# Threshold attention and a GELU feed-forward on one core: the last six token blocks by 49 products, eight blocks in pairs, merged additions, and one written order for every task

## The chip, the cores and the metric

The kernel runs on one core of a Trainium2 chip. The core has five engines with a queue of instructions each: TensorE (PE, the matrix multiplications; the loading of its weights is shown apart, as PEld), VectorE (DVE), ScalarE (ACT), GpSimd (POOL) and SyncE (SP, which here only starts transfers). The engines run side by side and wait for each other by semaphores; 16 DMA engines move data. The metric is the time of one execution on the device in microseconds (us).

## The reference

All numbers are 32-bit floats. Attention with a threshold is followed by a feed-forward:

```python
q, k, v: (8, 8, 576, 64)                     # batch, heads, positions, head size
scores = scale * q @ k.T                     # per batch and head: 576 x 576
keep   = scores >= max(scores, row) - tau    # everything else gets -1e9
attn   = exp(kept scores - max) / (sum + 1e-9)
x = (attn @ v)  as  (4608 tokens, 512)       # 8 batches x 576 positions, 8 heads x 64
h = x @ w_in                                 # w_in  512 x 2048
g = h * sigmoid(1.702 * h)
out = g @ w_out                              # w_out 2048 x 512
```

## The kernel before

**Attention.** Two heads of a batch are done together, so there are 32 "pairs" n (4 per batch). Each uses the four quarters of TensorE's array, 64 rows by 64 columns, for four small multiplications side by side. Pair n runs through these steps (functions of the code, whose lines are listed below): `load_qk`, `load_v` (transfers); `prep` (DVE transposes of q and k, L556); `scores` (PE, 9 groups of four 64x288 matmuls); `keep` (ACT copies the scores from PSUM to SBUF, L607) into five tiles t = 0 to 4, four of 128x1152 numbers and a last one of 128x576; `in_groups` (DVE maximum, L613), `over_tiles`, `cross_max` (ACT), `over_halves` and `spread_max`, which end in the row maximum spread over a tile called `mb`; `sub` (DVE subtracts `mb` from each of the five tiles, L687); `mask` and `exps` (ACT, L694 and L698); `in_groups` again for the sums; `values` (PE, L709); and `place_x` (DVE, L813), which divides by the sums and writes the pair's part of x, transposed, to the tile `xT`. The `values` of one pair and the `scores` of the next are interleaved on PE tile by tile in a run of about 8 us. In pairs 1 and 3 to 6 the subtraction of tiles 3 and 4 is not done by DVE but by a transfer that adds as it writes (`add_row`, L678), issued on POOL's queue.

**Feed-forward.** The 4608 tokens are 18 blocks of 256, numbered 0 to 17 here. Blocks 0 and 1 are done plainly. Others use Strassen's scheme: a product of two 2x2 block matrices takes seven products P1 to P7 instead of eight, at the price of additions of quarters of the operands and of the results.

- `seven` (blocks 2 to 6, and 13): first layer `product1` (L954), matmuls with 128 columns; each result of a half y is kept by ACT (`keep1`) or added by DVE (`add1`), and `silu1` (ACT) follows.
- `seven4` (blocks 7 to 12, in pairs, since two blocks share a weight): `product4` (L1127) with 256 columns, `keep4` (L1168), `add4` (L1173), `silu4`. The sums of weights that it needs are kept in DRAM (`wrow`) and are brought into four places in turn by transfers on POOL's queue (`w_flow`, L1104).
- Second layer of all of these: `product` (L1431), 256 columns, with sums of g made by DVE (`s_sums`, `s_minus`, `s_last`), and results read by `read` (ACT, L1446) and added into `osb` by DVE (L1453).
- `tail_blocks` (blocks 14 and 15, then 16 and 17): the scheme is applied twice, 49 products for each layer and pair of blocks, 128 columns each: `product2` (L1278) and `product3` (L1387). The 49 weights are sums made earlier on DVE (`scrap_sum`, named in EARLY_EXTRAS and LATE_EXTRAS) and written to DRAM (`ext`, `exu`), from where SP brings them back in time (`extra_in`, `extra2_in`).

**Order.** The program is built as a list of tasks (engine, cost, rank, what must be done first, places taken and given back). `run_in_order` goes through simulated time: whenever an engine is free it takes the ready task with the lowest rank. Feed-forward tasks on PE have the rank LAST, so attention comes first where it can; the others have ranks by pair, shifted by tables of numbers (EARLY, SECOND, LATER, CV). `limits` gives how many buffers of a kind there are. LEAD = 8 keeps pair n from starting before task `ffn[16 * (n - 8)]` of the feed-forward. What comes out is a fixed queue of instructions for each engine.

## Time and profile before

| what | value |
|---|---|
| time, median of 3 runs | 1224.76 us (1223.8 to 1225.64) |
| profiled execution: span | 1224.7 us |
| PE busy | 1206.5 us (99%) |
| DVE busy | 1077.1 us (88%) |
| ACT busy | 797.6 us (65%) |
| POOL busy | 69.3 us (6%) |
| mean traffic with memory | 111 GB/s |
| PE clock granted | full from the second 50 us on, 0.97 in the first |

The profile is that of one execution; its span is the time of that execution, and it lies at the median of the runs to 0.1 us. A busy share is a mean over stages with different limits, so the page's numbers are read stage by stage. A row of the groups ("by line") reads: line, engine, operation, output<-input with their shapes, how many, then busy us and mean ns of one, then the idle time of the engine just before them and what ended it. A row of windows gives the stretch, its length, each engine's busy us with the number of instructions, the clock, the busy share of the DMA engines and GB/s.

### The profile page before, as it was taken

Reading aid. Unit: us, or ns where it says so; the run is one execution under the profiler, and the core shown is the slowest. Engines: PE = TensorE matmul, PEld = TensorE weight load, DVE = VectorE, ACT = ScalarE, POOL = GpSimd, SP = SyncE. Lnnn points to the kernel's source line nnn. Section 1 sums busy time; section 2 is a strip of 40 time slices with the busy share of each in tenths; the row PEclk is TensorE's granted clock in tenths of the full one; section 3 lists DMA queues with packets and bytes.
Section 4 is the critical chain, followed back from the end, with each engine's and each line's share of the span. In section 5 each row is a group of like instructions: output and inputs, shape, how many; then the busy total and the mean of one; then the engine's idle time right before and its main releaser. Section 6 shows DMA issues by size and latency. Waiting matters only on the chain.

```text
span 1224.7 us, 26240 instructions
## 1 busy us (share of the span) xinstructions
PE 1206.5 (99%) x10672; PEld 995.8 (81%) x10672; DVE 1077.1 (88%) x1683; ACT 797.6 (65%) x1197; POOL 69.3 (6%) x114
## 2 busy tenths in 40 slices
PE   8999999999999999999999999999999999999998
PEld 5656777797978888888777777787787797999998
DVE  6989998878898998898699977998799989999797
ACT  6999977675765766684686468756875676340340
POOL 0111231100000000000100010001100000000000
PEclk9999999999999999999999999999999999999999
DMA  8957769492323241224423252225322351444443
GB/s 222 249 108 190 173 142 170 103 210 65 93 50 110 49 120 48 75 72 135 101 67 99 66 133 72 59 77 128 92 49 67 87 139 39 139 129 140 140 137 104
DMA packets 201193, 136.09 MB, mean 111 GB/s; under 512 B 146864, under 2 KB 163376, under 8 KB 200944
## 3 DMA queue, kind: packets, MB, share of 16 engines
q1 hardware_dynamic: 189712, 110.21, 34.0%
q0 software_dynamic: 10672, 23.90, 9.4%
q8 instruction: 84, 1.38, 0.5%
q10 hardware_dynamic: 688, 0.30, 0.1%
q14 instruction: 37, 0.30, 0.1%
HBM read 103.28 MB, written 23.75 MB: 104 GB/s over the span
## 4 chain that ended last, share of the span: by engine, by line
PE 88%; ACT 8%; DMA 2%; DVE 1%; issue 1%; SPq 0%; DVEq 0%; ACTq 0%
PE ops L1431 28%; PE pv L709 10%; PE ps L590 10%; PE hps L954 7%; PE hps L1127 7%; PE ps L954 5%; PE ps L1127 5%; PE hps L1278 4%; PE ops L1387 4%; PE ps L1278 3%; PE ps L1387 3%; ACT arena L698 2%; ACT arena L694 2%; PE hps L886 2%; ACT arena L607 2%; DMA arena<-in_moe_w_in_dram 1%
## 5 line engine op out<-in xcount | busy, mean ns | idle before, releaser
L613 DVE TRANSPOSE_TENSOR_REDUCE part<-arena 128x36 f32<-128x1152 f32 x300 | 363.8, 1239 | 52.6 <-ACT arena L607 40.2
L607 ACT COPY arena<-ps 128x576 f32<-128x576 f32 x288 | 171.2, 642 | 95.6 <-PE ps L590 95.5
L694 ACT ACTIVATE arena<-arena 128x1152 f32<-128x1152 f32 (+1 forms) x160 | 164.6, 1064 | 66.6 <-DVE arena L687 66.2
L1431 PE MATMUL ops<-w_out,arena 128*128 128x256 f32 x896 | 203.0, 381 | 0.1
L1431 PEld LDWEIGHTS ops<-w_out,arena 128*128 128x128 f32 x896 | 168.5, 190 | 28.5 <-issue 5.3
L687 DVE TENSOR_TENSOR arena<-arena 128x1152 f32<-128x1152 f32 (+1 forms) x150 | 180.9, 1241 | 0.7
L698 ACT ACTIVATE arena<-arena,shift 128x1152 f32<-128x1152 f32 (+1 forms) x160 | 179.7, 1156 | 1.4
L590 PE MATMUL ps<-arena 64*64 64x288 f32 x2304 | 172.1, 408 | 8.0 <-ACT arena L607 6.1
L709 PE MATMUL pv<-arena 64*64 64x288 f32 x2176 | 159.2, 405 | 0.0
L590 PEld LDWEIGHTS ps<-arena 64*64 64x64 f32 x2304 | 81.9, 132 | 71.5 <-ACT arena L607 29.7
L1431 PE MATMUL ops<-arena 128*128 128x256 f32 x576 | 129.1, 379 | 0.0
L709 PEld LDWEIGHTS pv<-arena 64*64 64x64 f32 x2176 | 80.3, 133 | 53.0 <-issue 9.0
L1431 PEld LDWEIGHTS ops<-arena 128*128 128x128 f32 x576 | 109.2, 190 | 15.8 <-issue 0.9
L1292 ACT COPY arena<-hps 128x512 f32<-128x512 f32 x44 | 25.7, 584 | 59.5 <-PE hps L1278 59.5
L632 ACT ACTIVATE other<-red,minus_gap 32x18 f32<-32x18 f32 x118 | 36.2, 307 | 35.1 <-DVE red L622 33.6
L1104 POOL DMA_DIRECT2D arena<-wrow x36 | 19.5, 540 | 619.0 <-DVE arena L1197 321.8
L886 PE MATMUL hps<-xT,w_in 128*128 128x256 f32 x232 | 51.2, 381 | 0.9 <-DVE arena L892 0.9
L886 PEld LDWEIGHTS hps<-xT,w_in 128*128 128x128 f32 x232 | 43.6, 190 | 8.6 <-DVE arena L892 1.5
L1453 DVE SCALAR_TENSOR_TENSOR osb<-ops,osb 128x256 f32<-128x256 f32 x98 | 39.2, 411 | 11.5 <-PE ops L1431 10.5
L954 PEld LDWEIGHTS hps<-xT,w_in 128*128 128x128 f32 x384 | 44.2, 192 | 1.5 <-issue 0.9
L954 PE MATMUL hps<-xT,w_in 128*128 128x128 f32 x384 | 45.3, 276 | 0.0
L1127 PE MATMUL hps<-xT,w_in 128*128 128x256 f32 x192 | 43.4, 379 | 0.0
(228 smaller groups left out, 1859.9 us busy)
## 6 DMA issues: line engine op xcount, KB each, us to landing
arena<-in_v_dram SPq DMA_DIRECT2D x128, 144.0 KB
arena<-exu SPq DMA_DIRECT2D x42, 256.0 KB
arena<-ext SPq DMA_DIRECT2D x39, 256.0 KB
arena<-wrow POOLq DMA_DIRECT2D x36, 256.0 KB, 3.3
arena<-in_k_dram SPq DMA_DIRECT2D x112, 72.0 KB
arena<-in_q_dram SPq DMA_DIRECT2D x112, 72.0 KB
out_dram<-osb SPq DMA_DIRECT2D x28, 256.0 KB
arena<-row_s SPq DMA_DIRECT2D x48, 144.0 KB
```

Of the source, the lines that this page charges most:

```text
L590: nc.tensor.matmul(ps[ts(c, KT), h, 0:SH], lhsT=mats[n, 1][ts(h, D), ts(j, KT)], rhs=mats[n, 0][ts(h, D), ts(c, SH)], start=True, stop=True,)
L607: nc.scalar.copy(out=sT[n, t][:, u], in_=pss.pop((n, j))[:, :, 0:SH])
L613: nc.vector.tensor_reduce(out=stats[n, op][:, t * 2 * QB : min(2 * t + 2, NK) * QB], in_=sT[n, t].rearrange("p u h (g d) -> p (u h g) d", ...
L687: engine.tensor_tensor(out=s, in0=s, in1=mbs[n].unsqueeze(1).to_broadcast(list(s.shape)), op=ALU.add if n in BY_DMA else ALU.subtract,)
L694: nc.scalar.activation(out=s, in_=s, func=AF.Prelu, alpha=STEEP)
L698: nc.scalar.activation(out=s, in_=s, func=AF.Exp, scale=SCALE, bias=shift)
L709: nc.tensor.matmul(o[c][ts(h, D), 0:SH], lhsT=left(j, h)[ts(c, KT)], rhs=sT[n, t][ts(c, KT), u, h, :], start=(j == 0), stop=(j == NK - 1),)
L886: nc.tensor.matmul(hidden[j][:, ts(i, BLK)], lhsT=w_in[:, c, ts(j, P)], rhs=xTs[i][:, c, :], start=(c == 0), stop=(c == NDC - 1), skip_gro ...
L954: nc.tensor.matmul(o[:, ts(j, HT)], lhsT=left[:, c, ts(4 * y + j, P)], rhs=right[:, c, :], start=(x in (P1, P2, P5) and j + c == 0), stop= ...
L1127: nc.tensor.matmul(o[:, ts(j, BLK)], lhsT=left[:, c, ts(j, P)], rhs=right[:, c, :], start=(x in (P1, P2, P5) and j + c == 0), stop=(j + c ...
L1278: nc.tensor.matmul(o[:, ts(j, HT)], lhsT=left[:, ts(j, P)], rhs=right, start=(m in (P1, P2, P5) and j == 0), stop=(j == 3), skip_group_che ...
L1431: nc.tensor.matmul(banks[blk][k][:, ts(o, HM)], lhsT=left[:, j, :], rhs=right[:, j, :], start=(j == 0), stop=(j == HF - 1),)
```

## The change

What it does, part by part:

1. **The tail grows from four blocks to six.** TAIL is NBLK - 6, so blocks 12 to 17 form three pairs with 49 products per layer. All three are created after the last pair of heads. x of blocks 12 to 15 is written to DRAM (`x_out`, on SP's queue) when it is complete and fetched back (`x_in`, SP) before its pair of blocks begins.
2. **Blocks 4 to 11 go in pairs** (`seven4`): WIDE_AT is (4, 6, 8, 10). Only blocks 2 and 3 remain with `seven`. EARLY_EXTRAS and LATE_EXTRAS spread the same 42 sums of weights over other blocks.
3. **P7 comes before P5** in the first layer (ORDER7), so that P4 stands between P5 and P3.
4. **Additions are merged.** `add1`, `add4`, `s_sums`, `s_next`, `s_minus`, `s_last`, `s_second` work on both halves at once (128x1024 instead of two of 128x512); `prep` transposes q and k at once; in pairs from 7 on the sums of tiles 1 and 2 come from one instruction; P4 is kept by an ACT copy like P1, P6 and P7, and all of a layer's silu come together at its end, 1024 wide.
5. **Pairs 7 to 31 leave the subtraction of tiles 3 and 4 to transfers.** The maximum is made negative (NEGATED), and `add_mb` issues on POOL's queue two transfers per pair that add `mb` (in SBUF) to tile 3 (576 KB) and tile 4 (288 KB).
6. **Buffers and gates.** The spread sums of pairs 7 to 31 have a place of their own ("rc2"); LEAD is NP, so that gate never closes; `values` may begin after two tiles' exps for all pairs after 7.
7. **A place for every task.** PLACES holds 4767 numbers, a permutation, one for each task; in `run_in_order` it replaces every rank. Pools and dependencies work as before.

Where the queues move, PE first: the start of a pair of blocks in the first layer, with a run of the attention (L709 and L590 before, L983 and L839 now). `hps` and `ps` are results in PSUM; a row with `x8` is one product of a half. Before:

```order
L1127 MATMUL hps<-xT,w_in 128x256 x8
L1127 MATMUL ps<-xT,w_in 128x256 x8
L1127 MATMUL hps<-arena_90,arena 128x256 x8
L709 MATMUL pv<-arena_90 64x288 x8
L590 MATMUL ps<-arena_90 64x288 x8
```

```order
L590 MATMUL ps<-arena_90 64x288 x4
L1127 MATMUL ps<-arena_90,arena 128x256 x8
L1127 MATMUL hps<-xT,w_in 128x256 x8
L1127 MATMUL hps<-arena_90,w_in 128x256 x8
L1127 MATMUL ps<-xT,arena 128x256 x8
```

Now (L1411 is `product4`):

```order
L1411 MATMUL hps<-xT,w_in 128x256 x8
L1411 MATMUL ps<-xT,w_in 128x256 x8
L1411 MATMUL hps<-arena_90,arena 128x256 x8
L1411 MATMUL hps<-xT,w_in 128x256 x8
L983 MATMUL pv<-arena_90 64x288 x8
L839 MATMUL ps<-arena_90 64x288 x8
```

P6 and P7 (the third and fourth row, both into `hps`) now follow each other, as P7 and P4 did before; the run of the attention stands one product later.

Then DVE in one pair's softmax, from `over_halves` on. Before, the five `sub` (L687) stand among the additions of the second layer (L1453) and `place_x` (L813):

```order
L639 SCALAR_TENSOR_TENSOR red<-red,gap,other_83 128x18
L651 STREAM_TRANSPOSE arena_90<-red 128x576
L687 TENSOR_TENSOR arena_90<-arena_90 128x1152
L1453 SCALAR_TENSOR_TENSOR osb<-ops,osb 128x256
L687 TENSOR_TENSOR arena_90<-arena_90 128x1152
L813 TENSOR_TENSOR xT<-pv,arena_90 128x128
L813 TENSOR_TENSOR xT<-pv,arena_90 128x160
L813 TENSOR_TENSOR xT<-pv,arena_90 128x96
L813 TENSOR_TENSOR xT<-pv,arena_90 128x192
L1453 SCALAR_TENSOR_TENSOR osb<-ops,osb 128x256 x2
L687 TENSOR_TENSOR arena_90<-arena_90 128x1152 x2
L687 TENSOR_TENSOR arena_90<-arena_90 128x576
```

Now (L961 is `sub`, L1458 `add4`, L879 `in_groups`, L869 the merged `sums_in_groups`):

```order
L906 SCALAR_TENSOR_TENSOR red<-red,gap,other_83 128x18
L919 STREAM_TRANSPOSE arena_90<-red 128x576
L961 TENSOR_TENSOR arena_90<-arena_90 128x1152 x3
L879 TENSOR_REDUCE part<-arena_90 128x36
L1458 TENSOR_TENSOR arena_90<-ps,arena_90 128x1024
L869 TENSOR_REDUCE part<-arena_90 128x72
L879 TENSOR_REDUCE part<-arena_90 128x36
L1458 TENSOR_TENSOR arena_90<-ps,arena_90 128x1024
L879 TENSOR_REDUCE part<-arena_90 128x18
```

Three `sub` remain, and the sums of tiles 1 and 2 are one row with 72 results.

And POOL in the second half of the program. Before, it holds only the stream of weight sums:

```order
L1104 DMA arena<-wrow_92 128x512 x2
L1104 DMA arena<-wrow_91 128x512 x2
L1104 DMA arena<-wrow_93 128x512 x2
L1104 DMA arena<-wrow_92 128x512 x2
```

Now (L1388 is `w_flow`, L954 `add_mb`):

```order
L954 DMA arena_90<-arena_90 128x2x576
L954 DMA arena_90<-arena_90 128x576
L1388 DMA arena<-wrow_92 128x512 x2
L1388 DMA arena<-wrow_91 128x512 x2
L954 DMA arena_90<-arena_90 128x2x576
L954 DMA arena_90<-arena_90 128x576
L1388 DMA arena<-wrow_93 128x512 x2
L1388 DMA arena<-wrow_92 128x512 x2
```

Each pair's two transfers now stand in the same queue as the weight sums.

The core of the diff (line numbers of the changed file differ from those of the profile before):

```diff
+    PLACES = """
+        114 170 133 238 4 92 157 188 151 49 8 600 155 191 299 353 83 365 180 203 376 143 354 391 326 212
...
+    """.split()
     def run_in_order():
+        for i, place in enumerate(PLACES):
+            tasks[i] = (*tasks[i][:2], int(place), *tasks[i][3:])
...
-    def prep(n, which):
-        dst = home(n, f"qkT{which}")
-        nc.vector.transpose(out=dst, in_=raws.pop((n, which)))
+    def prep(n):
+        (src, _), (dst, _) = room["raw0"][0], room["qkT0"][0]
+        nc.vector.transpose(out=arena2[:, dst : dst + 2 * S], in_=arena2[:, src : src + 2 * S])
...
+    def sums_in_groups(n, t):
...
+        lo, mid, size = held[n, t][1], *held[n, t + 1][1:]
...
+        nc.vector.tensor_reduce(
+            out=stats[n, ALU.add][:, t * 2 * QB : min(2 * t + 4, NK) * QB],
+            in_=arena2[:, lo : mid + size].rearrange("p (c d) -> p c d", d=32),
+            axis=AXL.X, op=ALU.add, apply_transpose=True,
+        )
...
+            negate=op == ALU.max and n in NEGATED,
...
-            op0=ALU.subtract, op1=ALU.max,
+            op0=ALU.add if n in NEGATED else ALU.subtract,
+            op1=ALU.min if n in NEGATED else ALU.max,
...
+    def add_mb(n, t):
+        s = sT[n, t].rearrange("p u h s -> p u (h s)")
+        nc.gpsimd.dma_start(
+            out=s, in_=mbs[n].unsqueeze(1).to_broadcast(list(s.shape)), accum_op=ALU.add
+        )
     def sub(n, t):
...
-            op=ALU.add if n in BY_DMA else ALU.subtract,
+            op=ALU.add if n in BY_DMA or n in NEGATED else ALU.subtract,
...
+    def x_out(blk):
+        x_rows[blk] = dram.tile([P, NDC * BLK], FP32, name=f"xrow{blk}", tag=f"xrow{blk}", bufs=1)
+        nc.sync.dma_start(out=x_rows[blk], in_=x_flat(blk))
+        del xTs[blk]
+    def x_in(blk):
+        xTs[blk] = work.tile([P, NDC, BLK], FP32, name="xT", tag="xT", bufs=NXT)
+        nc.sync.dma_start(out=x_flat(blk), in_=x_rows[blk])
...
-    TAIL = NBLK - 4
+    TAIL = NBLK - 6
...
-    WIDE = 7
-    WIDE_AT = (7, 9, 11)
+    WIDE = 4
+    WIDE_AT = (4, 6, 8, 10)
...
     def keep4(q, x):
-        f, h = {P1: (0, 0), P6: (0, 1), P7: (1, 1)}[x]
+        f, h = {P1: (0, 0), P6: (0, 1), P7: (1, 1), P4: (1, 0)}[x]
         nc.scalar.copy(out=quarter4(q, f, h), in_=in_twos(bank1(x, q % 2)))
-    def add4(q, x):
+    def add4(z, x):
         f, h = {P2: (0, 0), P5: (1, 1), P3: (0, 1)}[x]
-        o = quarter4(q, f, h)
-        nc.vector.tensor_tensor(out=o, in0=in_twos(bank1(x, q % 2)), in1=o, op=ALU.add)
...
+        o = (g, g1)[h][:, f, ts(z, 4), :]
+        ps = places["p2" if x == P2 else "p5"].rearrange("p y (j t) -> p (y j) t", t=BLK)
+        nc.vector.tensor_tensor(out=o, in0=ps, in1=o, op=ALU.add)
+    def silu4(z, f, h):
+        o = (g, g1)[h][:, f, ts(z, 4), :]
+        nc.scalar.activation(out=o, in_=o, func=AF.Silu, scale=GELU_SCALE)
...
-    ADDED = {n: (3, 4) for n in (1, *range(3, 7))}
+    ADDED = {n: (3, 4) for n in (1, *range(3, NP))}
     BY_DMA = (1, *range(3, SINGLE))
+    NEGATED = range(SINGLE, NP)
     SUMS_BY_DMA = range(4, NP)
-    LEAD = 8
+    LEAD = NP
...
+    ORDER7 = (P1, P2, P6, P7, P5, P4, P3)
+    LATE_SILU = True
...
-        for x in (P1, P2, P6, P5, P7, P4, P3):
+        for x in ORDER7:
...
-    EARLY_EXTRAS = {
-        3: ((0, P6), (0, P5)), 4: ((0, P3), (0, P1)), 5: ((0, P2), (1, P1)), 6: ((1, P2), (1, P6)),
-    }
+    EARLY_EXTRAS = {2: ((0, P6), (0, P5)), 3: ((0, P3), (0, P1))}
...
-    LATE_EXTRAS = {7: ((0, P4), (1, P4)), 9: ((0, P7), (1, P7)), 11: ((1, P5), (1, P3))}
+    LATE_EXTRAS = {4: ((0, P2), (0, P4), (1, P4)), 6: ((1, P1), (1, P2), (1, P6)), 8: ((0, P7), (1, P7)), 10: ((1, P5), (1, P3))}
...
             if next_blk >= TAIL:
-                if (next_blk - TAIL) % 2:
-                    tail_blocks(next_blk - 1)
+                pass
...
+        if n == NP - 1:
+            for blk in range(TAIL, NBLK, 2):
+                tail_blocks(blk)
...
+    EARLY_SUMS = 1
+    PAIRED = (1,)
...
-                    after=exped[m][: BEGUN if n > SECOND_RC else NKT + 1] + exped[m][NKT + 1 :] + [loaded[m], pq, pk] + after
+                    after=exped[m][: BEGUN if n > SINGLE else NKT + 1] + exped[m][NKT + 1 :] + [loaded[m], pq, pk] + after
```

More of the change, by code (lines that the diff above doesn't have):

```diff
@@ L213 @@
     }
+    AT = {
[24 rows of a table added]
+    }
+    FFI = set()
+    FFR = {
+        "add1": 0.0,
+        "add4": 0.0,
+        "keep1": 0.0,
+        "keep4": 0.0,
+        "read": 0.0,
+        "s_last": 0.0,
+        "s_minus": 0.0,
+        "s_next": 0.0,
+        "s_sums": 0.0,
+        "scrap_sum": 0.0,
+        "silu1": 0.0,
+        "silu4": 0.0,
+        "x_sum": 0.0,
+        "x_sum0": 0.0,
+        "x_sum3": 0.0,
+    }
+    STEP = {
+        "add_mb": 0.0,
+        "exps": 0.0,
+        "in_groups": 0.0,
+        "keep": 0.0,
+        "mask": 0.0,
+        "sub": 0.0,
+    }
     CV = {
@@ L1652, in feed_forward @@
         ys = [done[0:4], done[4:8]]
[L1653 to L1655 removed]
+        second(blk, {P1: ys, P2: ys, P4: ys}, *left_tasks(blk, ys[0] + ys[1]))
     last1 = []
@@ L2123, in seven4 @@
+            if LATE_SILU:
+                last = task("ACT", 0.93, FIRST, silu4, z, 0, 1, after=[made[z][1][P3], last])
+                gs[0, 1][z] = last
         for (q, x), k in turn.items():
@@ L2267, in second @@
             if x == P6:
-                lasts = [task("DVE", 0.6, FIRST, s_last, blk, k, after=ffn[-1:]) for k in range(2)]
+                lasts = task("DVE", 1.24, FIRST, s_last, blk, after=ffn[-1:])
             if x == P1:
```

395 lines of the change are left out of this document (199 added, 196 removed), and 207 rows, old and new, of tables (AT, PLACES).

## The prediction

> **What bounds the kernel now.** I read the page's first parts, then the windows by stage, the chain of waits, the groups by shape and the waits.
>
> ```profile
> span 1224.7 us, 26240 instructions
> PE 1206.5 (99%) x10672; PEld 995.8 (81%) x10672; DVE 1077.1 (88%) x1683; ACT 797.6 (65%) x1197; POOL 69.3 (6%) x114
> core 0: us, PE busy (x) PEld busy (x) DVE busy (x) ACT busy (x) POOL busy (x), PEclk, DMA share, GB/s
> 0.00:50.00 50.00, 43.26 (x672) 30.57 (x676) 38.11 (x54) 39.76 (x62) 7.60 (x23) 0.97 0.94 251
> 50.00:100.00 50.00, 46.19 (x632) 27.04 (x628) 43.65 (x74) 49.34 (x66) 5.87 (x8) 1.00 0.65 145
> 100.00:150.00 50.00, 45.85 (x375) 33.34 (x368) 46.92 (x76) 48.14 (x76) 14.32 (x20) 1.00 0.71 165
> 150.00:200.00 50.00, 49.80 (x347) 39.77 (x349) 46.01 (x72) 39.27 (x53) 12.39 (x15) 1.00 0.83 161
> 200.00:600.00 400.00, 400.00 (x3559) 333.94 (x3552) 347.84 (x503) 263.14 (x388) 14.08 (x20) 1.00 0.39 98
> 600.00:1046.00 446.00, 445.90 (x3542) 355.87 (x3541) 393.52 (x557) 305.13 (x451) 15.04 (x28) 1.00 0.33 83
> 1046.00:1134.00 88.00, 88.00 (x788) 87.97 (x787) 85.25 (x188) 27.43 (x54) 0.00 (x0) 1.00 0.48 145
> 1134.00:1222.00 88.00, 87.50 (x784) 87.31 (x782) 75.82 (x165) 25.35 (x51) 0.00 (x0) 1.00 0.43 127
> ```
>
> From 200 us to the end PE is busy for 1021.4 of 1022 us, so the time there is PE's work; only the first 200 us hold 14.9 us without it (200 less 43.26, 46.19, 45.85 and 49.80). The sum goes against the profiled 1224.7 us, which stands at the median of the runs (1224.76). What counts is how many matmuls go, at which spacing, and whether DVE, the second fullest, still keeps up. The spacing stands in the chain of waits; the timeline gives the tail's start and end.
>
> ```profile
> 244.53 3.57 PE hps L954 x32
> 573.09 3.45 PE hps L1127 x16
> 729.73 6.91 PE hps L1127 x32
> 958.35 15.74 PE ops L1431 x72
> 1046.16 1.05 PE L1278 MATMUL hps<-xT,w_in 128*128 128x128 f32 x8
> 1220.45 1.06 PE L1387 MATMUL ops<-arena,arena 128*128 128x128 f32 x8
> ```
>
> A 128-column matmul takes 3.57/32 = 0.1116 us, one with 256 columns 3.45/16 = 0.2156.
>
> **PE's work (parts 1 and 2 of the change).** One block by `seven` is 224 matmuls of 128 columns and 112 of 256: 25.0 + 24.15 = 49.1 us. A `seven4` pair is 448 of 256 columns, 96.6 us, 48.3 a block. A tail pair is 784 of 128 columns, 87.5 by the spacing; measured, the two pairs run from 1046.16 to 1221.5 us, 87.7 each, and that is taken.
>
> - Blocks 4 to 7 were three `seven` and half a pair, 147.4 + 48.3 = 195.7 us; as two pairs they are 193.2: -2.5.
> - Blocks 12 and 13 were half a pair and one `seven`, 48.3 + 49.1 = 97.4; as a tail pair 87.7: -9.7.
> - Blocks 0 to 3, 8 to 11 and 14 to 17, and the attention, keep their matmuls: 0. PE's stream changes between attention and feed-forward as often as before (69 times): 0.
>
> PE loses 12.2 us. Against that spacing speaks a rule of the Trainium skill, "TensorE: Matmul & The Clock Gate", section on the back-to-back issue gap: sustained matmuls of 128 columns come every 81 ns or so, while its formula for an isolated one gives 109 at 256. By that ratio of 0.74 (an estimate from that page) a tail pair would take 784 x 0.74 x 0.2156 = 125 us. The two measured spacings stand as 0.52 and the tail's pairs took 87.7 us, so the trace disagrees.
>
> **DVE in the middle (parts 4, 5, 6).** Six blocks now wait for the end and LEAD no longer holds pairs back, so the attention of pairs 7 to 21 has less feed-forward between its runs. I counted the queues between the first scores of the eighth pair and of the 22nd, at the durations by shape.
>
> ```profile
> 196.00:686.00 490.00, 489.97 (x4232) 405.68 (x4228) 427.73 (x616) 328.42 (x482) 16.23 (x24) 1.00 0.38 95
> 900.00:1000.00 100.00, 100.00 (x843) 81.69 (x842) 91.60 (x129) 69.22 (x101) 0.00 (x0) 1.00 0.33 85
> L687 DVE TENSOR_TENSOR arena<-arena 128x1152 f32<-128x1152 f32 x123 | 162.2, 1349 | 0.7
> L687 DVE TENSOR_TENSOR arena<-arena 128x576 f32<-128x576 f32 x27 | 20.2, 749 | 0.0
> L613 DVE TRANSPOSE_TENSOR_REDUCE part<-arena 128x36 f32<-128x1152 f32 x240 | 321.7, 1362 | 50.0 <-ACT arena L607 37.5 <-ACT arena L698 11.6
> L1173 DVE TENSOR_TENSOR arena<-ps,arena 128x512 f32<-128x512 f32 x36 | 23.7, 685 | 20.6 <-PE ps L1127 19.8
> L1017 DVE TENSOR_TENSOR arena<-w_out 128x1024 f32<-128x1024 f32 x2 | 2.4, 1218 | 0.0
> L694 ACT ACTIVATE arena<-arena 128x1152 f32<-128x1152 f32 x128 | 144.8, 1161 | 66.3 <-DVE arena L687 66.2
> L698 ACT ACTIVATE arena<-arena,shift 128x1152 f32<-128x1152 f32 x128 | 157.1, 1253 | 1.3
> L698 ACT ACT_TABLE_LOAD x14 | 18.0, 1283 | 0.3
> ```
>
> Before, PE's matmuls there add up to 467.9 us and the stretch lasts 490 (the first row): 22.1 go to the turns into and out of 14 runs. After, they add up to 365.1, with the same turns 387 us. DVE's instructions add up to 382.7, times 0.929 (DVE's busy time over the same sum before, since neighbours overlap) 355 us, 92% of that; ACT's come to 295, 76%. DVE was 87.3% busy in the stretch (427.73 of 490) and 91.6% between 900 and 1000 us with PE full, and 85.25 of 88 in the tail. So 92% is a little past what the attention has shown: at a share of 91.6% the stretch takes 387.6 us, no loss; if DVE can't pass 87.3%, 407, +20. I take +2, near the first, since it is a share at which PE was seen full, and keep +20.
>
> What makes DVE lighter: merging two additions saves 2 x 685 - 1218 = 152 ns each. Two `sub` per pair go in 25 pairs: 25 x (1.349 + 0.749) = 52 us of DVE. ACT loses 16 table loads (20.5 us) and gains copies in place of silu from PSUM. None of it was on the chain for long, so by itself it is worth 0: it pays for the 92%.
>
> **The transfers that add (part 5).** A wait is added: `mask` of tiles 3 and 4 waits for a landing instead of a `sub`. Behind it on ACT stand the exps, on PE the values.
>
> ```profile
> arena<-row POOLq DMA_DIRECT2D x10, 288.0 KB, 7.6
> arena<-wrow POOLq DMA_DIRECT2D x36, 256.0 KB, 3.3
> w_in<-w_in POOLq DMA_DIRECT2D x1, 1024.0 KB, 7.9
> arena<-w_out POOLq DMA_DIRECT2D x3, 1024.0 KB, 10.0
> L1104 POOL DMA_DIRECT2D arena<-wrow x36: 537/537/620, 568.2 to 884.4; - x36
> ```
>
> The last row is one group's durations in ns (least, median, most). The adding transfer of before, 288 KB, landed 7.6 us after issue; 1024 KB within SBUF took 7.9 to 10.0. So 576 KB should take 7.6 to 10.0, nearer the first, which has the same operation. In the order ACT has 1.35 us of wait for the first `sub` and three `mask` and `exps` of its own, 1.35 + 3 x (1.161 + 1.253) = 8.6 us, before it needs tile 3: cost 0. At 10.0 it is 1.4 us late in each of 25 pairs, 35 us if no feed-forward matmul fills the place. The `w_flow` transfers share the queue: an issue took 0.54 us, which delays the next by as much: 0, with 4 places filled ahead. The page "SBUF — State Buffer" of the Trainium skill (who interferes with whom) says that DVE operations with two SBUF inputs hold a port against GpSimd's reads. If that stretched the issues, the rows of `w_flow` would show it, and their most is 620 ns beside a DVE that is busy over 85%.
>
> **Order, tail and start (parts 3, 6, 7).** P7 right after P6 needs ACT's copy of P6 during one product of the other half; P7 and P4 stood so before, and the chain's third row shows 32 of their matmuls in 6.91 us, no gap: 0. The fetches of x for a tail pair: block 14's is issued 8.2 us of PE's work ahead of its use, block 15's 12.5.
>
> ```profile
> 136.82 7.41 DMA arena<-in_moe_w_out_dram
> PEld ps L590 <- ACT arena L607: 29.7, 65, 2.0
> ACT arena L607 <- PE ps L590: 95.5, 118, 6.4
> ```
>
> A load of 512 KB, as large as x of a block, took 7.41 us: 0, up to +3 if both are late. In the tail DVE fits (75.82 to 85.25 of 88 us for each pair). The last two rows show PE's weight loads and ACT waiting for each other in the score runs (us, times, longest): this is inside the 22.1 us of turns and stays: 0. The first 200 us are bound by loads and ACT; the order there has ACT at 179 us of work before the first `product` against 176: 0, between +3 and -14.9, all of PE's idle time.
>
> **The sum.** 1224.7 - 2.5 - 9.7 + 2 = 1214.5 us.
>
> **The rivals.**
> - *DVE becomes the bound in the middle.* For it: 92% against 87.3% as a mean. Against: 91.6% seen with PE full. It costs +6 to +20 on 1212.5: 1219 to 1232.
> - *The added transfers land late* (this one ends slower). For it: tile 3 is twice the 288 KB of the row, and 25 pairs depend on it. Against: the 1024 KB rows are hardly longer. Past 8.6 us each us costs 25: it decides from 0.5 us late (12.2/25), a landing of 9.1 us; at 10.0, 1214 + 35 = 1249. So 1225 to 1249.
> - *The start shrinks too.* The written order could close part of the 14.9 us. For it: every task is placed anew, and the softmax is lighter on DVE. Against: loads fill the DMA engines there (0.94 in the first 50 us). 1199 to 1208.
> - *The page's rule on 128 columns holds once three pairs stand in a row.* Moved blocks then cost 125 - 97.4 = +27.7 instead of -9.7, and the time is 1250. Against it stand two pairs in a row at 87.7 us.
>
> **How the numbers follow.** My forecast 0.60, its own range 1209 to 1218 (0 to 3 us for the fetches, 0 to +5 for DVE, some of the start back); DVE bound 0.17; late transfers 0.10; the start 0.12; the page's rule 0.01. The range runs from 1203, half of the start's case, to 1232, DVE's bound. A measurement of this kernel tells about 0.2% (2.4 us) from no change, so faster ends at 1222.3: 0.60 + 0.12 + 0.05 of DVE's case = 0.77; same 0.05 from DVE's case; slower 0.07 + 0.10 + 0.01 = 0.18.
>
> **What would show it.** Right: three tail pairs of 87.7 us; PE busy about 1194 us and its idle time still near 18; the rows of ACT's `mask` without long waits for the added transfers; those transfers landing in 7 to 9 us; DVE above 90% in the middle. Wrong: PE idle between 200 us and the tail, ended by ACT's exps or by DVE (DVE's bound), `mask` waiting for a transfer (late landing), or 128-column matmuls spaced above 0.112 us.

## The result

The changed kernel takes 1219.35 us (median of 5 runs, 1216.12 to 1220.53) against 1225.64 us for the kernel before beside it: a ratio of 0.9948 with an interval of 0.993 to 0.9966, some 6 us faster. A second set of runs on another occasion (below) gave 0.9951 (0.9938 to 0.9963). The forecast was faster, 1214.5 us, in a range of 1203 to 1232; the gain is about six tenths of the 10.2 us that the sum gave, and the time lies 1.4 us above the likeliest case's own range (1209 to 1218).

The page's first lines, and the windows by stage. The stages end at the first scores of the eighth pair, at those of the 22nd, and at the first matmul of the tail; the last three rows lie in the three tail pairs. The changed kernel:

```profile
span 1218.7 us, 26167 instructions
PE 1196.9 (98%) x10560; PEld 982.3 (81%) x10560; DVE 1067.9 (88%) x1622; ACT 794.1 (65%) x1183; POOL 130.5 (11%) x176
core 0: us, PE busy (x) PEld busy (x) DVE busy (x) ACT busy (x) POOL busy (x), PEclk, DMA share, GB/s
0.00:191.50 191.50, 176.65 (x1924) 122.13 (x1928) 170.40 (x256) 173.56 (x248) 40.49 (x66) 0.99 0.76 183
191.50:584.80 393.30, 390.09 (x3436) 307.10 (x3432) 354.60 (x455) 295.38 (x424) 51.83 (x62) 1.00 0.65 148
584.80:952.10 367.30, 367.01 (x2860) 290.31 (x2853) 305.00 (x393) 247.31 (x355) 38.16 (x48) 1.00 0.51 122
956.00:1044.00 88.00, 88.00 (x791) 88.00 (x790) 80.39 (x179) 26.59 (x53) 0.00 (x0) 1.00 0.54 167
1044.00:1132.00 88.00, 88.00 (x789) 87.86 (x788) 80.20 (x177) 25.79 (x53) 0.00 (x0) 1.00 0.48 139
1132.00:1218.00 86.00, 83.23 (x746) 83.04 (x744) 73.92 (x160) 24.31 (x50) 0.00 (x0) 1.00 0.41 122
```

The kernel before, cut at the same places:

```profile
0.00:196.00 196.00, 181.09 (x1944) 128.17 (x1948) 171.38 (x266) 173.74 (x248) 40.18 (x66) 0.99 0.78 180
196.00:686.50 490.50, 490.47 (x4240) 406.00 (x4236) 428.23 (x616) 328.42 (x482) 16.23 (x24) 1.00 0.38 94
686.50:1046.00 359.50, 359.43 (x2932) 286.37 (x2925) 316.43 (x451) 242.62 (x362) 12.89 (x24) 1.00 0.33 84
```

To compare stages that hold different work, I priced PE's matmuls in each trace at their undisturbed spacing (0.216 us for 256 columns, 0.112 for 128, 0.0525 for one of the attention's, which run side by side; the start holds some 350 smaller ones besides, the same in both kernels) and took the rest of the stage as lost: turns, waits and a lower clock together.

| stage | before: us, matmuls, lost | after: us, matmuls, lost | change of matmuls, of the lost |
|---|---|---|---|
| to pair 7's scores | 196.0, 161.5, 34.5 | 191.5, 156.3, 35.2 | -5.2, +0.7 |
| middle, 14 pairs | 490.5, 468.0, 22.4 | 393.3, 365.1, 28.2 | -102.9, +5.8 |
| from there to the tail | 359.7, 341.0, 18.7 | 367.3, 348.8, 18.6 | +7.8, -0.1 |
| tail | 175.1, 175.6, -0.5 | 262.8, 263.4, -0.6 | +87.8, -0.1 |
| sum | | | -12.5, +6.3 |

So PE's matmuls fell by what was forecast (12.5 us for 12.2), and the middle gave 5.8 us back. The sum of the two changes, -6.2, is that of the spans, 1224.7 to 1218.7, but for 0.2.

Where the middle's 5.8 us lie shows in what PE and its weight loads waited for there (us in total, times, longest). After:

```profile
PE ps L839 <- ACT arena L856: 2.8, 4, 0.9
PEld ps L839 <- ACT arena L856: 11.6, 26, 1.4
```

Before, where PE itself waited for nothing in the middle, and its weight loads for ACT's copy L607 (now L856):

```profile
PEld ps L590 <- ACT arena L607: 6.8, 19, 0.5
```

It is ACT's copy of the scores that comes late, in a few runs of scores and values, and hardly DVE (one wait of 0.4 us). By the windows PE is idle for 3.2 us of the middle, against 0.03 before; with 1.7 us of a lower clock (below) that is 4.9 of the 5.8 us, and what the rest is stays open. The largest of these waits, in the timeline (start, duration, then what it is; in brackets the wait ahead):

```profile
355.53 2.00 ACT L1263 ACTIVATE arena<-arena 128x1024 f32<-128x1024 f32 x2
...
358.49 1.04 ACT L1263 ACTIVATE arena<-arena 128x1024 f32<-128x1024 f32 x1
...
359.55 1.28 ACT L972 ACT_TABLE_LOAD   x1
360.84 1.26 ACT L972 ACTIVATE arena<-arena,shift 128x1152 f32<-128x1152 f32 x1
362.00 0.62 ACT L856 COPY arena<-ps 128x576 f32<-128x576 f32 x1
362.52 1.16 ACT L968 ACTIVATE arena<-arena 128x1152 f32<-128x1152 f32 x1
362.68 0.72 PE L839 MATMUL ps<-arena 64*64 64x288 f32 x8 [0.88 <-ACT arena L856]
363.59 0.63 ACT L856 COPY arena<-ps 128x576 f32<-128x576 f32 x1
364.27 1.07 PE L839 MATMUL ps<-arena 64*64 64x288 f32 x8 [0.88 <-ACT arena L856]
```

The first rows are the last of block 3's silu, which all stand at the end of its layer; then ACT loads the exp's table and does an exps of the pair before, and the copy that frees a PSUM buffer waits behind them. PE stands still twice.

What follows such a place is the second finding. In this profile the granted clock falls behind two stalls:

```profile
92.00:96.00 4.00, 1.21 (x16) 0.50 (x12) 4.00 (x5) 3.20 (x3) 0.00 (x0) 0.86 0.95 325
96.00:100.00 4.00, 4.00 (x56) 2.14 (x52) 3.97 (x5) 3.93 (x5) 0.00 (x0) 0.72 0.32 73
360.00:364.00 4.00, 2.51 (x40) 1.04 (x32) 3.88 (x3) 3.99 (x5) 0.00 (x0) 1.00 0.00 0
364.00:368.00 4.00, 3.73 (x36) 2.13 (x40) 4.00 (x4) 3.02 (x5) 0.00 (x0) 0.57 0.01 2
```

At 0.57 for 4 us PE loses another 1.7 us, as much as it stood. In the whole profile these are the only two places with a lower clock.

### The profile page after: what moved, and what is told of

Read it like the earlier page. It is cut to its first block, busy times and chain, and to the rows that moved or that the text cites. A ratio compares the mean times of both kernels' runs of the same rounds, so it can differ in the third digit from the quotient of the medians.

```text
span 1218.7 us, 26167 instructions
## 1 busy us (share of the span) xinstructions
PE 1196.9 (98%) x10560; PEld 982.3 (81%) x10560; DVE 1067.9 (88%) x1622; ACT 794.1 (65%) x1183; POOL 130.5 (11%) x176
## 4 chain that ended last, share of the span: by engine, by line
PE 78%; ACT 14%; DVE 3%; DMA 3%; issue 2%; POOL 0%; SPq 0%; DVEq 0%; ACTq 0%; POOLq 0%
PE ops L1719 21%; PE pv L983 9%; PE ps L839 8%; PE hps L1411 8%; PE hps L1566 6%; PE ops L1675 6%; PE ps L1411 6%; PE ps L1566 5%; PE ps L1675 5%; ACT arena L968 4%; ACT arena L972 3%; ACT arena L856 2%; PE hps L1238 2%; PE ps L1238 1%; DVE arena L961 1%
## 5 line engine op out<-in xcount | busy, mean ns | idle before, releaser
L879 DVE TRANSPOSE_TENSOR_REDUCE part<-arena 128x36 f32<-128x1152 f32 (+1 forms) x250 | 297.3, 1212 | 21.4 <-ACT arena L856 15.0
L856 ACT COPY arena<-ps 128x576 f32<-128x576 f32 x288 | 171.5, 643 | 54.6 <-PE ps L839 52.1
L839 PE MATMUL ps<-arena 64*64 64x288 f32 x2304 | 172.7, 409 | 7.8 <-ACT arena L856 6.2
L1719 PE MATMUL ops<-w_out,arena 128*128 128x256 f32 x768 | 174.6, 381 | 0.8 <-DVE osb L1741 0.4
L1719 PEld LDWEIGHTS ops<-w_out,arena 128*128 128x128 f32 x768 | 144.4, 190 | 26.9 <-issue 4.8
L983 PE MATMUL pv<-arena 64*64 64x288 f32 x2176 | 160.4, 407 | 0.0
L839 PEld LDWEIGHTS ps<-arena 64*64 64x64 f32 x2304 | 81.9, 133 | 70.9 <-ACT arena L856 29.1
L961 DVE TENSOR_TENSOR arena<-arena 128x1152 f32<-128x1152 f32 (+1 forms) x100 | 130.1, 1337 | 2.9 <-DMA arena<-row 2.2
L983 PEld LDWEIGHTS pv<-arena 64*64 64x64 f32 x2176 | 81.1, 133 | 52.7 <-issue 7.9
L1580 ACT COPY arena<-hps 128x512 f32<-128x512 f32 x66 | 38.5, 583 | 114.3 <-PE hps L1566 114.2
L1719 PE MATMUL ops<-arena 128*128 128x256 f32 x464 | 104.4, 380 | 0.7 <-ACT osb L1734 0.7
L954 POOL DMA_DIRECT2D arena<-arena x50 | 55.1, 1317 | 429.2 <-DVE arena L919 245.1
L869 DVE TRANSPOSE_TENSOR_REDUCE part<-arena 128x72 f32<-128x2304 f32 x25 | 64.2, 2570 | 10.8 <-ACT arena L972 10.5
L1411 PE MATMUL hps<-xT,w_in 128*128 128x256 f32 x256 | 59.4, 382 | 0.1
L1411 PEld LDWEIGHTS hps<-xT,w_in 128*128 128x128 f32 x256 | 48.1, 190 | 9.4 <-issue 2.6
L1452 ACT COPY arena<-hps 128x512 f32<-128x512 f32 x64 | 36.8, 578 | 26.7 <-PE hps L1411 26.5
L899 ACT ACTIVATE other<-red,gap 32x18 f32<-32x18 f32 x100 | 30.7, 307 | 35.9 <-DVE red L888 34.7
```

Source lines behind the costliest of these rows:

```text
L839: nc.tensor.matmul(ps[ts(c, KT), h, 0:SH], lhsT=mats[n, 1][ts(h, D), ts(j, KT)], rhs=mats[n, 0][ts(h, D), ts(c, SH)], start=True, stop=True,)
L856: nc.scalar.copy(out=sT[n, t][:, u], in_=pss.pop((n, j))[:, :, 0:SH])
L869: nc.vector.tensor_reduce(out=stats[n, ALU.add][:, t * 2 * QB : min(2 * t + 4, NK) * QB], in_=arena2[:, lo : mid + size].rearrange("p (c d ...
L879: nc.vector.tensor_reduce(out=stats[n, op][:, t * 2 * QB : min(2 * t + 2, NK) * QB], in_=sT[n, t].rearrange("p u h (g d) -> p (u h g) d", ...
L961: engine.tensor_tensor(out=s, in0=s, in1=mbs[n].unsqueeze(1).to_broadcast(list(s.shape)), op=ALU.add if n in BY_DMA or n in NEGATED else A ...
L983: nc.tensor.matmul(o[c][ts(h, D), 0:SH], lhsT=left(j, h)[ts(c, KT)], rhs=sT[n, t][ts(c, KT), u, h, :], start=(j == 0), stop=(j == NK - 1),)
```

## The experiments

Times are compared by the ratio to the kernel before, since the sets were run on different occasions (its median was 1224.18, 1224.36 and 1224.35 us in the three sets). "After" is the changed kernel, 0.9948 and 0.9951.

**The changed kernel again.** No edit; it stood beside the last three kernels.

> The changed kernel once more, beside the three below, so that these are compared on one chip and with their own runs of the kernel before: 1217 to 1221, 5 to 7 us below the kernel before. If it lies at 0.997 of the kernel before, the runs with other orders (1219.9 to 1220.7) were no slower than it.

Measured: 1218.76 us (1217.2 to 1220.23), 0.9951 (0.9938 to 0.9963). In its profile the middle takes 392.5 us with 27.4 lost, 5.0 more than before, at full clock throughout: the loss is there without a lower clock too.

**The order by ranks, and with it a tail of four blocks.** For the first, the table of places is empty:

```diff
     PLACES = """
-        114 170 133 238 4 92 157 188 151 49 8 600 155 191 299 353 83 365 180 203 376 143 354 391 326 212
...
     """.split()
```

and for the second, besides:

```diff
-    TAIL = NBLK - 6
+    TAIL = NBLK - 4
-    WIDE_AT = (4, 6, 8, 10)
+    WIDE_AT = (4, 6, 8, 10, 12)
...
-8: ((0, P7), (1, P7)), 10: ((1, P5), (1, P3))}
+8: ((0, P7), (1, P7)), 10: ((1, P5), (1, P3)), 12: ()}
```

> The changed kernel with the table of places left empty, so that the ranks set the order again; the matmuls and all other instructions are the same. Theory (PE's matmuls set the time, the order only the turns and stalls): PE's sum stays, the idle time grows by some us: 1220 to 1235. Rival (the written places are what pays, the lighter PE would be lost without them): above 1235.

> Like the kernel with ranks only, but with a tail of four blocks: blocks 12 and 13 as a pair with seven products instead of two levels. Theory: a pair takes 96.6 us by seven products and 87.7 in the tail, so 8.9 us more than with ranks only. Rival (the third tail pair waits for its loads or for DVE, so that it isn't worth its matmuls): less than 4 us more, or a gain.

With ranks only: 1222.45 us, 0.9986 (0.9977 to 0.9995), inside the theory's range. PE's matmuls are those of the changed kernel in each stage (156.3, 365.1, 348.8, 263.4 us); lost were 30.4, 29.6, 22.1 and 1.2 us. So the written places are worth about 4 us by the ratios, and 2.0 by the spans of the two profiles. By these they win 1.4 us in the middle, 3.5 behind it and 1.8 in the tail, and lose 4.8 in the start, which was better with ranks.

With four blocks in the tail: 1243.06 us, 1.0157 (1.0142 to 1.0171), 20.6 us more than with ranks only, where 8.9 were expected. By stages the matmuls are 96.7 us more ahead of the tail and 87.8 less in it: the 8.9 us are there. The other 11 or so are lost in the tail (11.9 us against 1.2), where PE and its weight loads wait for ACT's copies, and PE as long for results on DVE (two windows, then the longest two waits):

```profile
1050.00:1100.00 50.00, 44.55 (x380) 42.89 (x379) 39.22 (x77) 17.32 (x31) 0.00 (x0) 1.00 0.48 149
1100.00:1150.00 50.00, 46.77 (x409) 45.82 (x408) 45.32 (x107) 8.92 (x23) 0.00 (x0) 1.00 0.44 132
```

```profile
PEld hps L1382 <- ACT arena L1396: 4.9, 5, 1.3
PE hps L1382 <- ACT arena L1396: 3.9, 5, 1.1
```

8.7 us of 100 are without PE: 3.9 us of waits for ACT's copies of `hps`, 0.8 for other results of ACT and 3.9 for DVE's. The term of the sum is confirmed, by count and spacing; that more than the term is lost besides was not foreseen. The order was not fitted to this tail, which is the likely reason, but it was not tried apart.

**DVE's load.** The subtraction of tiles 3 and 4, or of tile 4 alone, back on DVE, straight behind that of tile 2; everything else in each queue as it was:

```diff
     def add_mb(n, t):
+        pass
-        s = sT[n, t].rearrange("p u h s -> p u (h s)")
-        nc.gpsimd.dma_start(
-            out=s, in_=mbs[n].unsqueeze(1).to_broadcast(list(s.shape)), accum_op=ALU.add
-        )
...
             op=ALU.add if n in BY_DMA or n in NEGATED else ALU.subtract,
         )
+        if n in NEGATED and t == 2:
+            sub(n, 3)
+            sub(n, 4)
```

(for tile 4 alone, `add_mb` returns only where `t == NKT`, and only `sub(n, 4)` is called).

> The changed kernel with the subtraction of tiles 3 and 4 of pairs 7 to 31 back on DVE, straight behind that of tile 2; the rest of each queue is as it was. DVE gains 2.1 us per pair, 27 us in the middle stretch (355 to 382 of 393 us, 97%) and 21 behind it. Theory (DVE can be at most about 92% busy beside a full PE): the middle grows to 382/0.916 = 417 us, the whole to about 1243. Rival (PE stays the bound up to a full DVE): 1219 to 1223. Second rival (the traffic of the added transfers is what the middle lost): below 1217.

> The changed kernel with the subtraction of tile 4 alone (128x576, 0.75 us) back on DVE in pairs 7 to 31, behind that of tile 2; tile 3 stays with the transfer. DVE gains 19 us against 52 when both go back, which cost 12 us. Theory (each us of DVE costs about a quarter, by stalls at many places): +4 to +5. Rival (a threshold: nothing as long as DVE is below some 93% in the middle): within 1.5 us.

Both tiles: 1231.7 us, 1.006 (1.0046 to 1.0073), by the ratios 13 us more than the changed kernel and 7 more than the kernel before. Tile 4 alone: 1218.75 us, 0.9957 (0.9943 to 0.9972), nothing that can be told from the 0.9951 beside it. The middle of the two, tile 4 alone first:

```profile
190.00:584.00 394.00, 389.93 (x3434) 307.43 (x3433) 363.81 (x470) 293.48 (x423) 38.66 (x48) 1.00 0.60 137
```

```profile
190.50:590.60 400.10, 390.74 (x3440) 305.20 (x3436) 379.37 (x483) 295.46 (x424) 21.60 (x34) 1.00 0.46 113
```

At 363.8 of 394 us (92.3%) DVE costs nothing, at 379.4 of 400.1 (94.8%) 6.8 us in the middle, and 4.3 behind it. So all three expectations of the first run were off: the bound by 91.6% (+24) was too strict, "up to a full DVE" too free, and without the transfers' traffic nothing was gained. With both tiles on DVE, PE waits in the middle 4.7 us for results on DVE (0.4 in the changed kernel) and 4.3 for ACT's copy (2.8). For the second run the threshold was right. That DVE's share sets it, and not where the subtractions stand in an order made without them, was not tried apart. The transfer of tile 4 could be left out at no cost here.

**Merged additions written as halves**, at the same places (as an example one of them; the others alike):

```diff
-        nc.vector.tensor_tensor(out=o, in0=ps, in1=o, op=ALU.add)
+        for y in range(2):
+            o_y = o[:, ts(y, 2), :]
+            nc.vector.tensor_tensor(out=o_y, in0=ps[:, ts(y, 2), :], in1=o_y, op=ALU.add)
```

> The changed kernel with each merged addition on DVE (prep, add1, add4, the sums of g and of tiles 1 and 2) written as two halves at the same place of the queue: some 130 instructions more, 0.06 to 0.15 us each, 8 to 20 us of DVE. Theory (DVE costs through stalls at a few places, about a quarter of what it gets more, as the subtraction on DVE cost 12 us for 48): +2 to +5. Rival (merging is worth nothing by itself): within 1 us.

1220.47 us, 0.9964 (0.9951 to 0.9977). That is 1.6 us above the changed kernel by the ratio, with intervals that overlap: between the two expectations, and it can't be told from nothing. DVE's busy time rose by 7.2 us (1067.9 to 1075.1), less than the 8 to 20 expected, and in its profile the middle took 392.9 us, no more than in the changed kernel's.

**Part 5 alone, in the kernel before.** The maximum of pairs 7 to 31 is made negative as in the change, and:

```diff
     def sub(n, t):
         s = sT[n, t].rearrange("p u h s -> p u (h s)")
+        if n >= SINGLE and t == 0:
+            for x in (3, 4):
+                s_x = sT[n, x].rearrange("p u h s -> p u (h s)")
+                nc.gpsimd.dma_start(
+                    out=s_x, in_=mbs[n].unsqueeze(1).to_broadcast(list(s_x.shape)), accum_op=ALU.add
+                )
+        if n >= SINGLE and t >= 3:
+            return
```

> The kernel before with part 5 alone: the maximum of pairs 7 to 31 negative, and the subtraction of tiles 3 and 4 by adding transfers issued where the first subtraction stood; nothing else moves. Theory (DVE is no bound before, its lightening is worth 0 by itself): 1221 to 1227, no difference. Rival (DVE's 2.1 us per pair are felt there too, a quarter of 52 us): 1212 or so. Second rival (the transfers stand behind the weight sums, which wait for PE on the same queue, and come late): above 1230.

1229.45 us, 1.0037 (1.002 to 1.0054): slower, which none of the three foresaw. In its profile 28.8 us are lost in the middle against 22.4, and 18.7 behind it as before. One place holds all of the 6.4: at 218 us PE waits for a read of ACT, and ACT for a store to the output, which frees its buffer.

```profile
ACT osb L1456 <- DMA out_dram<-osb: 6.7, 1, 6.7
PE ops L1441 <- ACT osb L1456: 3.3, 1, 3.3
```

The clock behind it:

```profile
218.00:222.00 4.00, 0.71 (x4) 0.30 (x2) 0.93 (x1) 0.58 (x2) 0.00 (x0) 0.86 1.08 255
222.00:226.00 4.00, 4.00 (x10) 3.19 (x11) 2.03 (x3) 4.00 (x5) 1.20 (x1) 0.50 0.26 45
226.00:230.00 4.00, 4.00 (x16) 3.38 (x15) 1.87 (x4) 4.00 (x5) 0.00 (x0) 0.78 1.05 184
```

A stall of 3.7 us and 2.9 us of lower clock. This profile is that of the slowest of seven runs: two, at a mean clock of 1.000, took 1224.9 and 1225.1 us, no more than the kernel before, and the other five, at 0.996 to 0.999, 1228.7 to 1233.3. So the loss comes and goes. 52 us less of DVE's work bought nothing that shows anywhere else, so the cost of 0 for the lightening by itself holds. That the added transfers made the store late is likely (the DMA engines are full in the row), but it was not tried apart.

**Later landings.** One, or four, more transfers per pair ahead of the two that add, to a scratch place in DRAM that nothing reads:

```diff
     def add_mb(n, t):
         s = sT[n, t].rearrange("p u h s -> p u (h s)")
+        if t == NKT - 1:
+            idle = dram.tile([P, 2, S], FP32, name="idle", tag="idle", bufs=2)
+            for _ in range(4):
+                nc.gpsimd.dma_start(out=idle, in_=mbs[n].unsqueeze(1).to_broadcast([P, 2, S]))
```

> The changed kernel with one more transfer per pair (mb written to a scratch place in DRAM, 576 KB) on POOL's queue ahead of the two that add; the computation is the same. The added tiles should land some 3 to 5 us later than the 6.7 us (median) measured, at 9.5 to 11.5. Theory of the prediction (8.6 us are covered, past that each us costs 25): +20 to +70 against the changed kernel. Rival (PE has other work to go on with and ACT is only three quarters busy, so a late tile is caught up): less than +10.

> As in the run with one more transfer ahead of the two that add, but with four. With one, mask of tile 3 began 6.0 to 18 us (median 6.9) after the issue, the tiles landed after 6.1 to 11.2, and nothing was lost. Four put about 5 us of POOL's issues and 2.3 MB of traffic ahead of the adding ones, so that tile 3 lands some 6 us later than mask wants it, in about 22 of 25 pairs. Theory of the prediction (each us past the cover costs 25): +100 or more. Rival (ACT, 75% busy, and PE, which has products to go on with, catch up on most of it): +10 to +50.

With one: 1220.53 us, 0.9973 (0.9958 to 0.9989), 2.7 us more than the changed kernel by the ratios, with intervals that overlap. The landing moved only from 6.7 to 7.9 us after the issue (median of both tiles), and ACT waited for it 1.4 us in all. This dose was too small to test the price. With four: 1494.68 us, 1.2197 (1.218 to 1.2213), 276 us more. Its span, its engines and four of its waits:

```profile
span 1489.2 us, 26340 instructions
PE 1250.5 (84%) x10560; PEld 1002.8 (67%) x10560; DVE 1072.3 (72%) x1622; ACT 797.9 (54%) x1183; POOL 199.9 (13%) x276
PE ps L839 <- ACT arena L856: 131.6, 27, 12.3
PE ps L1415 <- DMA arena<-wrow: 36.3, 4, 10.6
ACT arena L972 <- DMA arena<-arena: 247.3, 25, 12.9
POOL idle L957 <- DMA idle<-arena: 262.0, 72, 6.4
```

The four write the same place and so wait for each other (the last row), which made the delay 10 us and not the 6 I had meant. ACT waits 247.3 us, 25 times, and the span grows by 270.5: 1.09 us for each us of waiting. That this is so near the prediction's price is in part luck, for three things add up to it. PE waits 183 us for ACT in all, against 13 in the changed kernel, so about 0.7 us for each us of ACT's: part is caught up. It waits 47 us more for weight sums, which come by the same queue of POOL and which the price didn't have. And for the same matmuls PE is busy for 53.6 us longer (1250.5 against 1196.9), at a mean clock of 0.92. The rival (+10 to +50) falls all the same.

**The stall at 361 us.** PE's four next pieces of products moved ahead of that run; then, in the second kernel, also the two reads that they need, on ACT and DVE. The queue is collected before it is issued:

```diff
-                tasks[i][3](*tasks[i][4])
+                emitted.append(i)
...
+        begin = where(values, 12, [0])
+        sooner = [x for x in emitted[begin:] if tasks[x][3] is product][:4]
+        emitted[begin:] = sooner + [x for x in emitted[begin:] if x not in sooner]
+        for f, a, to, b in ((read, (3, 0), exps, (12, 2)), (read, (3, 1), sums_in_groups, (12, 1))):
+            i = emitted.pop(where(f, *a))
+            emitted.insert(where(to, *b) + 1, i)
+        for i in emitted:
+            tasks[i][3](*tasks[i][4])
```

(the first kernel has the same without the loop over `read`).

> The changed kernel with one move on PE: the run with pair 13's scores starts four pieces of products (24 + 12 matmuls, 5.2 us) later, so that ACT can finish the silu, the table load and two exps first. Theory (the middle lost 5.8 us to stalls in score runs): in the profile the two idle times of 0.88 us at 361 to 364 us and the clock of 0.57 behind them go away, -3.8 us in the profile (2.1 stalled, 1.7 for the clock); in the timed runs -2 to -4 against the changed kernel's 1219, since not each run need have had the dip. Rival (the loss is spread over all runs, or comes from the traffic of the added transfers): no change beyond 1 us.

> As in the run in which only PE's products of block 3 came sooner, and besides, the two reads that free their banks come sooner too: the one on ACT right behind the exps of tile 2, the one on DVE behind the merged sums of tiles 1 and 2. There the stalls at 361 to 364 us were gone, but two new ones (1.09 and 0.86 us) waited for these reads. Theory (the stalls come from ACT's and DVE's order at this place): neither the old nor the new ones show, the middle takes 390 to 392 us against 393.3, the whole 2 to 4 us less than the changed kernel. Rival (ACT is behind there, whatever the order, so the loss only moves): a stall of about 2 us shows somewhere within 30 us behind, and the time doesn't fall by more than 1 us.

1219.85 us, 0.9968 (0.9955 to 0.9981), and 1220.68 us, 0.9973 (0.9963 to 0.9984): neither is faster than the changed kernel. The stall at 361 us is gone in both but for one wait of 0.41 us. In the first, PE waits 15 us later for the read that stands behind all of ACT's copies:

```profile
375.76 0.39 ACT L1742 ACTIVATE osb<-ops 128x256 f32<-128x256 f32 x1
376.20 3.72 PE L1727 MATMUL ops<-arena 128*128 128x256 f32 x16 [1.09 <-ACT osb L1742]
```

In the second, that wait is gone, and PE waits 2 us for a read on DVE, which stands behind two subtractions and a sum of g:

```profile
376.86 2.63 DVE L976 TENSOR_TENSOR arena<-arena 128x1152 f32<-128x1152 f32 x2
379.40 1.22 DVE L1353 TENSOR_TENSOR arena<-arena 128x1024 f32<-128x1024 f32 x1
380.54 0.42 DVE L1756 SCALAR_TENSOR_TENSOR osb<-ops,osb 128x256 f32<-128x256 f32 x1
381.01 1.57 PE L1734 MATMUL ops<-arena 128*128 128x256 f32 x4 [2.05 <-DVE osb L1756]
```

My theory of a mendable place falls and the rival stands: what was taken from this place was owed at the next. Each engine's order was made for the others as they were, which is the likely reason. Whether the silu back at their old places, between the products, would have kept the copy in time was not tried.

**Ranks for the start, places from there on.**

```diff
+    FROM = 187.0
...
-        for i, place in enumerate(PLACES):
-            tasks[i] = (*tasks[i][:2], int(place), *tasks[i][3:])
+        places_of = [int(place) for place in PLACES]
...
-                for rank, i in queue if engine in MOVERS else sorted(queue):
+                for rank, i in queue if engine in MOVERS else sorted(
+                    queue, key=lambda y: y if now < FROM else (places_of[y[1]], y[1])
+                ):
```

> The changed kernel with the order by ranks for the first 187 us of the planner's time, and by the written places from there on; the instructions are the same. With ranks only, pair 7's scores began at 186.7 us against 191.5, the middle took 394.7 against 393.3, and what follows was slower by 5. Theory (the stages are independent: what the start gains is kept): 1213 to 1217, faster than both kernels. Rival (the places fit only the state that their own start leaves): 1218 to 1224, the gain given back in the middle.

1216.52 us (1215.27 to 1218.38), 0.9931 (0.9918 to 0.9945), against 0.9951 (0.9938 to 0.9963) for the changed kernel beside it. It is clearly faster than the kernel before. Against the changed kernel it is 2.2 us by the medians, with intervals that overlap, so probably faster, not surely. In its profile pair 7's scores begin at 187.0 us against 192.0 in the changed kernel beside it, the stage behind the middle loses the same 18.6, and the middle loses 30.6 against 27.4, with a lower clock behind the same stall in this profile (1.7 us). So of the 5.0 us won in the start 3.2 are given back there, about half of them by the clock, and 1.8 are kept: each expectation has a part.

## Why the prediction was right, and where it was off

- *PE's work, -2.5 and -9.7 us.* Right: 12.5 us in the stages, and 8.9 for the third tail pair in the kernel with four tail blocks. The tail's pairs take 87.6 us each (262.8/3), at 0.1117 us a matmul; also with three pairs in a row, so the rule of 81 ns (the Trainium skill, "TensorE: Matmul & The Clock Gate", back-to-back issue gap) does not hold for this stream.
- *The sum's base.* Off by 1.8 us: I set the span, 1224.7, equal to the time. In each listed run of the changed kernel the time is 1.8 to 1.9 us above the span (1220.53 and 1218.7, for one), so 1214.5 was a span, and the time that belongs to it 1216.3. The runs of the kernel before show the same difference, so its profiled execution took some 1226.5 us; that its span lay at the median of the times was chance.
- *DVE in the middle, +2.* This step failed. Its counts were right (355 us of DVE forecast and 354.6 measured, ACT 295 and 295.4, PE 365.1), and so was the reading that 92% of DVE costs PE nothing: with tile 4 back, 92.3% was no slower. What it missed was ACT: its 76% was taken as room, and the turns were kept at 22.1 us. ACT's copies came late in a few runs, and the middle lost 28.2 us instead of 22.4, of which PE's weight loads waited 4.8 us more for that copy. The term was mis-sized by 3.8 us, on another engine than the one it was for. The prediction had named PE's idle time between the start and the tail as a sign of being wrong: it came to 3.5 us (3.2 in the middle), where the kernel before had 0.1. That the time stays inside the range is owed to the range's width, which was made for DVE.
- *The transfers that add, 0.* Right. The 576 KB landed in 6.1 us (median), both tiles within 5.3 to 9.7 and so rather sooner than forecast, and no `mask` waited for them.

```profile
arena<-arena POOLq DMA_DIRECT2D x25, 576.0 KB, 6.1
arena<-arena POOLq DMA_DIRECT2D x25, 288.0 KB, 7.5
DMA to landing us min/median/max: 5.3/6.7/9.7
L1388 POOL DMA_DIRECT2D arena<-wrow x48: 537/557/1449, 389.3 to 876.4; - x48
```

  The price of lateness, 25 us per us, came out at 27 in the kernel with four more transfers (270.5 us for 9.9 in each pair), but by another sum: about 17 by ACT, and the rest by late weight sums and a lower clock. The last row is `w_flow` on the same queue: most issues took what they did before, some up to 1.45 us. The Trainium skill's page "SBUF — State Buffer" (who interferes with whom) says that a DVE instruction with two SBUF inputs contends with a GpSimd instruction that reads SBUF. Whether these issues are such reads no run here shows. No PE matmul waited for a weight sum in this trace; why some issues are long stays open.
- *P7 behind P6, fetches of x, tail: 0.* Right: no wait of PE names them, and the tail loses nothing (-0.6 us against the price).
- *The start, 0.* Right for this kernel (+0.7). That there was something to be had showed in the order by ranks, which loses 30.4 us there instead of 35.2: the rival in which the start shrinks names a real reserve, and the written places of the change go the other way; about 2 us of it could be kept in the last experiment.
- *The rivals.* DVE's load began to cost between 92.3 and 94.8% of the middle, in this order, and the change stays below that (90.2%, 354.6 of 393.3 us); late landing would have cost about what was said, though not all in the way that was said.

## What to carry to other kernels

When one engine is full and its work is cut, price the cut by matmuls and then look for the wait that ends last in the stretches where the rest is squeezed together; a mean share of 75% says little about an engine whose work comes in bursts, as ACT's four silu, table load, exps and copies here. An order fitted to all engines at once is hard to mend at one place by hand: in both tries here the debt moved. And a transfer that takes the place of an operation is free only as long as it lands inside its cover; past it, a good part of each us counted once per use here, and what shares its queue came late as well.

## What was not expected of the hardware

The granted clock fell behind stalls that were no more than 2 to 4 us, in one place with matmuls in between, and not each time. After 2.5 of 4 us busy it was 0.57 for 4 us in the changed kernel's profile; the same two waits of 0.88 us, in the kernel with halved additions, left it full:

```profile
358.00:362.00 4.00, 2.96 (x48) 1.31 (x40) 3.96 (x6) 3.97 (x5) 0.00 (x0) 1.00 0.02 4
362.00:366.00 4.00, 3.26 (x50) 1.71 (x54) 4.00 (x4) 4.00 (x8) 0.00 (x0) 1.00 0.00 0
366.00:370.00 4.00, 4.00 (x51) 2.57 (x44) 4.00 (x5) 3.02 (x6) 0.00 (x0) 1.00 0.13 33
```

Windows of 0.5 us show what the means over 4 us hide: in the changed kernel's profile the clock is 0.50 from 364.5 to 367.5 us and 1.00 on either side. The trace's record of the clock gives each of its two dips 3.413 us at one half, and their starts lie 269.65 us apart, 79 times 3.413; the dip in the kernel with part 5 alone is twice as long. So the profiles were cut into pieces of 3.413 us in step with these records. In the three profiles where a dip followed the two waits of 0.88 us (the changed kernel, tile 4 alone on DVE, ranks and then places), both lie in one piece, in which PE was busy for 0.48 to 0.49 of the time. In the four where none did (the changed kernel again, halved additions, one more transfer, both tiles on DVE), an edge cuts one of them, and PE was busy for 0.54 to 0.69 of the piece that holds the other. Over all 14 profiles a dip followed every piece at full clock in which PE was busy for less than 0.42, and none in which it was for more than 0.49. So the same stall is answered or not by how it falls into these pieces.

The Trainium skill's page "TensorE: Matmul & The Clock Gate" (the part on the clock gate) tells of an activity window of about 3.4 us that runs freely, so that the same program meets it in another phase each time. That agrees with dips of 3.413 us that come and go at one place; its advice to fear idle gaps longer than that window is too mild here, where two waits with work between them were enough. A dip costs some 1.7 us, as much as the stall. It may be part of why runs of one kernel differ by 4 us: two of the changed kernel's first five show a mean clock of 0.997 and 0.999 and spans of 1218.7 and 1217.7 us, and the three at 1.0 spans of 1214.3, 1214.7 and 1217.5. The second set doesn't bear that out: 1216.9 and 1218.4 us at 0.998, and 1215.4, 1215.9 and 1218.3 at 1.0.
